# Four first blocks over four pairs of loads, and an order planned with each pool tile's turn

## The chip, the cores and the metric

The kernel runs on one core of a Trainium2 chip. Its time is the device time of one execution, in microseconds (us). Five engines run their own instruction queues side by side: TensorE (PE, matrix products), VectorE (DVE) and ScalarE (ACT, both elementwise), GpSimd (POOL, almost unused here) and SyncE (SP), which here issues nearly all DMAs. A matmul reads two operands from the on-chip memory and accumulates into a bank of PSUM, 128 partitions of 512 floats.

## The reference

Two branches share their input and are mixed by a gate:

```python
    x = A_q
    g = _sigmoid((x * gate_w).sum(-1, keepdims=True))
    a = _A_ref(x, A_k, A_v, A_shift_k, A_ssm_k, A_ssm_D)
    b = _B_ref(x, B_w1, B_w2)
    return g * a + (1 - g) * b
```

Branch b is the dense one, relu(x w1) w2 for 2048 rows of 512 values, with an inner width of 1792. Branch a shifts k with four taps, multiplies it by v, convolves each channel over the whole sequence with `ssm_k` (by an FFT of twice the length), adds kv times `ssm_D` and multiplies by q. All is in 32-bit floats.

## The kernel before, in words

**Dense branch.** The rows are worked on in 4 chunks of 512, and the inner width in 14 blocks of 128. For chunk c and block f the first product ("m_c_f", 12 matmuls of 128x512, L353 to L355) goes to one of four shared PSUM banks, tag "cv". ACT takes the relu to a rounded high part hh (L365), DVE the rest hl (L368), which gives the bank free. The second product (12 matmuls, L380 to L382) adds to four banks of its own, m_c_0 to m_c_3, that are kept over the 14 blocks. For precision every operand is split: a copy to a rounded format is the high part (names with h, cast on ACT, L268), and what is left is the low part (names with l, DVE, L271); three matmuls (high by high, high by low, low by high) make one product. x, w1 and w2 are split on the chip, once for the weights.

**Head.** The blocks below G of chunk 0 are treated apart, since nothing is on the chip yet: their w1 columns come in an own array `wf` (`load_first`, L303, with casts gh at L316 and low parts gl at L319), and `mlp1_first` (L337) goes over the four pieces k of the 512 input values in the outer loop, so that it can start with the first piece of x and of weights. Thirteen matmuls on zeros (L737) run ahead of it. G is 2 before the change.

**Convolution.** It is a factored Fourier transform by small ("tiled") matmuls of 32 or 64 partitions. DVE forms the shifted k times v in tiles acc and tmp (conv_x); stage 1 (s1x of acc, s1h of the filter, L416, eight chunks each) fills all four "cv" banks in one run; ACT copies them to ev tiles (L426), which are stored and read back in another layout (r). In 8 rounds, the forward transforms f_h and f_x (L519) follow, then products on DVE in tiles z, u and xs (L533, copies L543), then the inverse iv (L613), again to four banks, copied by ACT to bv (L623), stored, read back, transformed once more (y, L714) and gated. These runs stand between dense matmuls.

**The order.** The program lists all operations with their engine, estimated duration, dependencies, rank, and what they take and give of each pool; `Plan.order` simulates the engines and always issues the ready operation of least rank. The kernel is emitted in that order, and each engine runs its own part of it strictly in that order. Room is a count by tag: an operation may be placed when enough tiles of its tag are free. The pool itself hands out the tiles of one tag in turn: the next tile is the one that has been given back longest ago in program order, and who takes it waits for that one's last user. Most work tiles (x, in, acc, tmp, ev, r, z, u, xs, bv, and so on) are one common tag, "a", 14 tiles of 128x1024 floats; the counts for ev, z and the others are caps on their share of it. A table of numbers sets the ranks, the pool sizes and caps, and margins (SAFE) that the planner adds to a time.

Of the kernel before, what the change touches and what calls it, by code (L numbers as in the profile page):

```python
# [8 lines left out]
F32 = mybir.dt.float32  # L9
F32R = mybir.dt.float32r  # L10
# [4 lines left out]
P = 128  # L15
# [64 lines left out]
class Plan:  # L80
# [3 lines left out]
    def __init__(self, room):  # L84
        self.room, self.ops, self.turn = dict(room), [], {}

# [13 lines left out]
    def order(self):  # L100
# [4 lines left out]
        out, soon, mode = [], [], False  # L105
# [9 lines left out]
        while True:  # L115
            for eng, ops in ready.items():
# [4 lines left out]
                if eng == "PE" and any(o["rank"][0] == 1 and not o["take"] for o in ops):  # L121
                    held = {"cv" for o in ops + (soon if SOON else []) if o["tiles"] and len(o["take"]) >= HOLD and all(self.turn[q][0] == o["n"] for q in o["fifo"])
                            and all(t == "cv" or self.room[t] >= o["take"].count(t) for t in o["take"])}
                for op in ops:
                    if best is not None and op["rank"] >= best["rank"]:
                        continue
                    if any(self.room[t] <= op["take"].count(t) - 1 for t in op["take"]):
                        continue
                    if any(self.turn[q][0] != op["n"] for q in op["fifo"]):
                        continue  # L130
                    if op["rank"][0] and any(t in held for t in op["take"]):
                        continue
                    if op["dma"] and pipe > now + DMA_AHEAD:
                        continue
                    best = op
# [4 lines left out]
                for t in op["take"]:  # L140
                    self.room[t] -= 1
                for q in op["fifo"]:
                    self.turn[q].pop(0)
# [20 lines left out]
            while events and events[0][0] <= now + 1e-9:  # L164
# [6 lines left out]
                if what == "done":  # L171
                    for t in op["give"]:
                        if isinstance(t, list):

                            t[0] -= 1
                            for name in () if t[0] else t[1:]:
                                self.room[name] += 1
                        else:
                            self.room[t] += 1
# [19 lines left out]
def act_time(n, psum=False):  # L199
    return n * 0.000833 + (0.17 if psum else 0.195)  # L200


def dve_time(n):
    return n * 0.001042 + 0.15
# [8 lines left out]
def build(tc, wf, xp, qn, kn, vn, hn, dn, sh, gw, w1, w2, cs1, ccc, cib, out):  # L213
# [20 lines left out]
    plan = Plan(room)  # L234
# [9 lines left out]
    def double(key, kind):  # L244
        T[key] = cpool[0].tile([P, 2 * D], F32, tag="a", bufs=AB, name=kind + "_" + "_".join(map(str, key)))
        return T[key]
# [56 lines left out]
    def load_first(ks, rank):  # L303
        n = G * P

        def load():
            w = double(("wf", ks[0]), "wf")
            nc.sync.dma_start(w[:, :len(ks) * n], wf[:, ks[0] * n:(ks[-1] + 1) * n])
            for i, k in enumerate(ks):
                T["g", k] = w[:, i * n:(i + 1) * n]  # L310

        ld = add("SP", ISSUE["SP"], rank, load, (), ["a", "ev"], dma=ROW * G // 4 * len(ks))
        free = [len(ks), "a", "ev"]
        for k in ks:
            def h(k=k):
                (nc.vector.tensor_copy if k == 0 else nc.scalar.copy)(tile_of(("g", "h", k), f"gh{k}", w=G * P, dt=F32R, p=wp), T["g", k])  # L316

            def l(k=k):
                nc.vector.tensor_tensor(tile_of(("g", "l", k), f"gl{k}", w=G * P, dt=F32R, p=wp), T["g", k], T["g", "h", k].bitcast(F32), op=OP.subtract)  # L319

            a = add("DVE", dve_time(G * P), -2000, h, [ld]) if k == 0 else add("ACT", act_time(G * P), -2000 + k, h, [ld])
            wdone["g", k] = add("DVE", dve_time(G * P), -2000 + k, l, [a], (), [free])
            wdone["gh", k] = a
# [6 lines left out]
    def mlp1_first():  # L330
        prev = [None] * G
        for k in range(4):
            for n, (a, b) in enumerate((("h", "h"), ("h", "l"), ("l", "h"))):
                for f in range(G):
                    def go(k=k, f=f, n=n, a=a, b=b):
                        ps = bank(("m1", 0, f)) if k == n == 0 else T["m1", 0, f]
                        mm(ps, part(a, f, k), T["x", b, 0, k], start=k == n == 0, stop=k == 3 and n == 2)  # L337

                    prev[f] = add("PE", MM, (1, -9, k, n), go, [(wdone["gh", k], xhigh[0, k]), (xdone[0, k],), (wdone["g", k],)][n] + (prev[f],),
                                  ["cv"] if k == n == 0 else ())  # L340
        for f in range(G):
            mlp1_out(0, f, prev[f])
# [400 lines left out]
    load_first((0,), -1002.5)  # L743
    load_first((1, 2, 3), -1001.5)
# [43 lines left out]
G = 2  # L788
# [7 lines left out]
SAFE = dict(PE0=0.3, PE1=0.175, ACT=0, DVE=0.4)  # L796
# [6 lines left out]
IN = 5  # L803
EV = 4
ACC = 2
TMP = 3
# [4 lines left out]
UB = 2  # L811
XSB = 1
CIB = 1
BVB = 3
EVI = [0, 0, 0, 0]
RK = {'H': -6, 'X': 4.5, 'Y': 0, 'I': 6}
HOLD = 4
SOON = 1
BRB = 6
QB = 2  # L820
# [3 lines left out]
EVR = 0  # L824
CWG = 8
# [3 lines left out]
BB = 3  # L829
X0 = -25.0  # L830
XP = 17.0
H0 = -20.0
# [43 lines left out]
```

## Time and profile before

Three runs took 405.32, 405.39 and 407.22 us, median 405.39. The profiled execution took 404.28 us by its own time; its span from first to last instruction is 402.1 us.

| what | value |
|---|---|
| span of the profiled execution | 402.1 us |
| its own time | 404.28 us |
| PE busy | 392.0 us (97%) |
| DVE busy | 287.7 us (72%) |
| ACT busy | 139.1 us (35%) |
| granted TensorE clock, mean | 0.999 |
| bytes moved by DMA | 93.52 MB, mean 233 GB/s |
| last dense product of the head (L337) ends, L353 starts | 12.43 us |
| last matmul starts | 398.03 us |

The names are the program's tiles, without buffer numbers. Busy times of PE overlap, since matmuls are pipelined: the distance between two starts is what one costs. "idle before <-" names what released an engine after it stood still.

### The profile page before, as it was taken

How to read it: one execution, taken by the hardware profiler on the slowest of the kernel's cores; microseconds unless marked ns; L12 is line 12 of the kernel's file. 1: busy time of each engine (PE TensorE's matmuls, PEld its weight loads, DVE VectorE, ACT ScalarE, POOL GpSimd, SP SyncE). 2: the span in 40 equal slices, each digit the busy share in tenths (PEclk: the TensorE clock that was granted, in tenths of full speed). 3: DMA queues.
4: the chain of work that ended last, by engine and by line, in shares of the span. 5: the costliest groups of instructions: out<-in, count | busy, mean ns of one | idle time of the engine just before them, and what ended most of it. 6: DMA issues, size and time to landing. Idle time of an engine off the chain costs nothing.

```text
span 402.1 us, 6451 instructions
## 1 busy us (share of the span) xinstructions
PE 392.0 (97%) x2509; PEld 268.3 (67%) x2509; DVE 287.7 (72%) x446; ACT 139.1 (35%) x263; POOL 1.4 (0%) x6
## 2 busy tenths in 40 slices
PE   7999999899999999999999999999998999999996
PEld 5878777578667666658556456474665786777774
DVE  4699999782897762279889797897989523664753
ACT  4553443344443343234343333323434520101110
POOL 0000000000000000000000000000000000000000
PEclk9999999999999999999999999999999999999999
DMA  7989668776677966674664829456393658987702
GB/s 253 373 311 332 224 213 297 266 256 253 210 261 260 343 253 221 225 291 128 223 174 166 269 89 300 121 217 182 148 251 149 210 164 316 387 319 282 261 0 104
DMA packets 39231, 93.52 MB, mean 233 GB/s; under 512 B 3841, under 2 KB 6289, under 8 KB 39202
## 3 DMA queue, kind: packets, MB, share of 16 engines
q1 hardware_dynamic: 39138, 93.08, 67.3%
q8 instruction: 19, 0.31, 0.3%
q0 software_dynamic: 64, 0.05, 0.1%
q14 instruction: 10, 0.08, 0.0%
HBM read 60.61 MB, written 32.51 MB: 232 GB/s over the span
## 4 chain that ended last, share of the span: by engine, by line
PE 90%; DMA 4%; DVE 2%; ACT 1%; SPq 1%; issue 1%; DVEq 0%; ACTq 0%
PE m L380 13%; PE m L353 13%; PE m L381 12%; PE m L382 12%; PE m L354 12%; PE m L355 12%; PE iv L613 3%; PE f_h L519 3%; PE f_x L519 3%; PE s1h L416 2%; PE y L714 2%; PE s1x L416 2%; DMA q_qs<-qn 2%; DMA wf_wf<-wf 1%; PE m L337 1%; DMA sa<-ev_evsh 1%
## 5 line engine op out<-in xcount | busy, mean ns | idle before, releaser
L380 PE MATMUL m<-w1h_h,hh 128*128 128x512 f32 x224 | 91.1, 407 | 0.0
L381 PE MATMUL m<-w1l_l,hh 128*128 128x512 f32 x224 | 87.5, 391 | 0.0
L382 PE MATMUL m<-w1h_h,hl 128*128 128x512 f32 x224 | 87.3, 390 | 0.0
L368 DVE SCALAR_TENSOR_TENSOR hl<-m,hh 128x512 fp32r<-128x512 f32 x56 | 38.6, 690 | 63.8 <-ACT hh L365 63.4
L365 ACT ACTIVATE hh<-m 128x512 fp32r<-128x512 f32 x56 | 33.4, 598 | 134.1 <-PE m L355 131.6
L353 PE MATMUL m<-xh_h,w0h_h 128*128 128x512 f32 x192 | 77.1, 402 | 2.0 <-ACT ev_evsx L426 1.6
L354 PE MATMUL m<-xl_l,w0h_h 128*128 128x512 f32 x192 | 75.0, 390 | 0.0
L355 PE MATMUL m<-xh_h,w0l_l 128*128 128x512 f32 x192 | 74.9, 390 | 0.0
L380 PEld LDWEIGHTS m<-w1h_h,hh 128*128 128x128 f32 x224 | 42.0, 188 | 34.7 <-issue 27.0
L353 PEld LDWEIGHTS m<-xh_h,w0h_h 128*128 128x128 f32 x192 | 36.0, 188 | 23.4 <-issue 6.7
L382 PEld LDWEIGHTS m<-w1h_h,hl 128*128 128x128 f32 x224 | 42.1, 188 | 9.0
L381 PEld LDWEIGHTS m<-w1l_l,hh 128*128 128x128 f32 x224 | 42.1, 188 | 7.5
L355 PEld LDWEIGHTS m<-xh_h,w0l_l 128*128 128x128 f32 x192 | 36.1, 188 | 7.7
L354 PEld LDWEIGHTS m<-xl_l,w0h_h 128*128 128x128 f32 x192 | 36.1, 188 | 6.8
L481 DVE TENSOR_TENSOR acc_acc<-acc_acc,tmp_tmp 128x1024 f32<-128x1024 f32 x24 | 29.4, 1224 | 0.7
L623 ACT COPY bv_bvs<-iv 128x512 f32<-128x512 f32 x30 | 15.7, 602 | 28.2 <-PE iv L613 16.1
L478 DVE TENSOR_TENSOR tmp_tmp<-in_k,sht_sht 128x512 f32<-128x512 f32 x32 | 21.3, 687 | 1.7 <-DMA in_k<-kn 1.6
L426 ACT COPY ev_evsx<-s1x 128x512 f32<-128x512 f32 x30 | 15.7, 599 | 18.9 <-PE s1x L416 16.1
L426 ACT COPY ev_evsh<-s1h 128x512 f32<-128x512 f32 x32 | 16.5, 601 | 13.3 <-PE s1h L416 10.6
L543 ACT COPY xs_xs<-f_x 128x512 f32<-128x512 f32 x24 | 13.5, 590 | 19.2 <-PE f_x L519 19.2
L533 DVE TENSOR_TENSOR z_pz<-f_x,z_hz 128x512 f32<-128x512 f32 x16 | 10.3, 687 | 11.8 <-PE f_x L519 11.8
L519 PE MATMUL f_x<-r_r_x,cw 64*32 64x512 f32 x256 | 16.7, 599 | 0.0
(70 smaller groups left out, 391.7 us busy)
## 6 DMA issues: line engine op xcount, KB each, us to landing
sa<-ev_evsh SPq DMA_DIRECT2D x16, 512.0 KB, 4.9
sa<-ev_evsx SPq DMA_DIRECT2D x16, 512.0 KB, 3.4
r_r_h<-sa SPq DMA_DIRECT2D x16, 512.0 KB, 5.7
r_r_x<-sa SPq DMA_DIRECT2D x16, 512.0 KB, 6.8
sb<-bv_bvs SPq DMA_DIRECT2D x32, 256.0 KB, 3.7
br_br<-sb SPq DMA_DIRECT2D x16, 512.0 KB, 6.7
raw<-w SPq DMA_DIRECT2D x26, 256.0 KB, 4.4
in_k<-kn SPq DMA_DIRECT2D x10, 512.0 KB, 6.4
```

The costliest lines, as they stand in the source:

```text
L353: mm(ps, part("h", f, k), T["x", "h", c, k], start=k == 0, stop=False)
L354: mm(ps, part("h", f, k), T["x", "l", c, k], start=False, stop=False)
L355: mm(ps, part("l", f, k), T["x", "h", c, k], start=False, stop=k == 3)
L365: nc.scalar.activation(tile_of(("hh", c, f), "hh", dt=F32R, p=mp, bufs=HHB), T["m1", c, f], AF.Relu)
L368: nc.vector.scalar_tensor_tensor(tile_of(("hl", c, f), "hl", dt=F32R, p=mp, bufs=HHB), T["m1", c, f], 0.0, T["hh", c, f].bitcast(F32), op0 ...
L380: mm(ps, T["hh", c, f][:, z], T["w", "h", 1, f], start=f == 0, stop=False)
L381: mm(ps, T["hh", c, f][:, z], T["w", "l", 1, f], start=False, stop=False)
L382: mm(ps, T["hl", c, f][:, z], T["w", "h", 1, f], start=False, stop=f == NF - 1)
L426: (nc.vector.tensor_copy if dve else nc.scalar.copy)(T["ev" + t, c, i], T["s1" + t, c, i])
L478: nc.vector.tensor_tensor(o[:, z], T["k", c + (j == 0) + part][:, u], T["sht", j // 2][:, j % 2 * D:(j % 2 + 1) * D], op=OP.mult)
L481: nc.vector.tensor_tensor(T["acc", c], T["acc", c], T[dst], op=OP.add)
L519: mm(ps[b][32 * j:32 * j + 32, :], T[k("cw")][at, 64 * j + 32 * o:64 * j + 32 * o + 32], T[k("r", t, j // 2)][at, (j % 2) * D:(j % 2 + 1) ...
```

## The change

Three things are changed.

1. `Plan` is given the list of tags that are only caps. For every other tag (the common pool "a", raw, x, hh, the PSUM banks and some more) it now keeps the tiles in the order in which the program gives them back. An operation is placed only when the tiles whose turn it is are free in the simulation (`fits`); before, any free tiles were enough.
2. The head takes four blocks (G = 4) in place of two. The weights come in four loads of 128x512 (256 KB), each following the load of the x piece that goes with it; before there were one of 128 KB and one of 384 KB. The first piece is cast on DVE in two halves. `mlp1_first` has 48 matmuls in place of 24, and in its last piece k = 3 it finishes block after block.
3. The table of numbers is another, and the order is planned anew with it. The numbers of dense and of small matmuls are the same as before (24 dense ones only move from `mlp1` to `mlp1_first`), and lines below `Plan` have moved: in the changed kernel the head's matmuls are L365, the first product L381 to L383, the second L408 to L410, s1x L444, f L547, iv L641, casts L291 and L294, gh L340, ev copies L454, bv copies L651.

```diff
+    def __init__(self, room, caps):
         self.room, self.ops, self.turn = dict(room), [], {}
+        self.tiles = {t: [[0]] * n for t, n in room.items() if t not in caps}
+
+    def fits(self, op, but=()):
+        for t in set(op["take"]) - set(but):
+            n = op["take"].count(t)
+            if self.room[t] < n or t in self.tiles and any(x[0] for x in self.tiles[t][:n]):
+                return False
+        return True
...
-                    if any(self.room[t] <= op["take"].count(t) - 1 for t in op["take"]):
+                    if not self.fits(op):
                         continue
...
                 for t in op["take"]:
                     self.room[t] -= 1
+                    if t in self.tiles:
+                        self.tiles[t].pop(0)
+                op["frees"] = []
+                for g in op["give"]:
+                    if isinstance(g, list):
+
+                        g[0] -= 1
+                        op["frees"].append(pending.setdefault(id(g), [0]))
+                        op["frees"][-1][0] += 1
+                        names = () if g[0] else g[1:]
+                    else:
+                        op["frees"].append([1])
+                        names = (g,)
+                    for t in names:
+                        self.room[t] += t in self.tiles
+                        op["frees"][-1].append(t)
+                        if t in self.tiles:
+                            self.tiles[t].append(op["frees"][-1])
...
-    plan = Plan(room)
+    plan = Plan(room, ("in", "acc", "tmp", "ev", "r", "z", "u", "xs", "bv", "br", "t", "b", "q"))
...
-    def load_first(ks, rank):
+    def load_first(k, rank):
         n = G * P
 
         def load():
...
+            T["g", k] = double(("wf", k), "wf")[:, :n]
+            nc.sync.dma_start(T["g", k], wf[k])
+
+        ld = add("SP", ISSUE["SP"], rank, load, (), ["a", "ev"], dma=ROW * G // 4)
+        parts = 2 if k == 0 else 1
...
-            for n, (a, b) in enumerate((("h", "h"), ("h", "l"), ("l", "h"))):
-                for f in range(G):
+            for n, f in [(n, f) for n in range(3) for f in range(G)] if k < 3 else [(n, f) for f in range(G) for n in range(3)]:
...
     for k in range(4):
         load_x(0, k, -1000 + k)
-    load_first((0,), -1002.5)
-    load_first((1, 2, 3), -1001.5)
+        load_first(k, -1002.5 + k)
...
-G = 2
+G = 4
...
-EVI = [0, 0, 0, 0]
+EVI = [0, 0, 0, 1]
...
-        "wf": w1[:, :, :G].transpose(1, 0, 2, 3).reshape(P, 4 * G * P),
+        "wf": w1[:, :, :G].reshape(4, P, G * P),
```

With EVI, one of the four bv copies of each of the first seven iv runs goes to DVE.

The order on SP at the start of the program, before (x_x is a piece of x, wf_wf of the first weights, raw a block of w1 or w2):

```order
L290 DMA x_x_0_76<-xp 128x512
L308 DMA wf_wf_78<-wf 128x256
L290 DMA x_x_1_94<-xp 128x512
L308 DMA wf_wf_96<-wf 128x768
L290 DMA x_x_2_98<-xp 128x512
L290 DMA x_x_3_102<-xp 128x512
L264 DMA raw_0_106<-w 128x512
```

and in the changed kernel:

```order
L313 DMA x_x_0_76<-xp 128x512
L331 DMA wf_wf_78<-wf 128x512
L313 DMA x_x_1_94<-xp 128x512
L331 DMA wf_wf_96<-wf 128x512
L313 DMA x_x_2_98<-xp 128x512
L331 DMA wf_wf_102<-wf 128x512
L313 DMA x_x_3_104<-xp 128x512
L287 DMA raw_0_110<-w 128x512
L287 DMA raw_1_116<-w 128x512
L287 DMA raw_2_123<-w 128x512
L331 DMA wf_wf_133<-wf 128x512
```

The first weights have grown from two loads to four, and the fourth stands behind three raw blocks.

The order on PE at the first s1x run of the program, before (the numbers in m_0_2 and m_0_3 with w1 are the second product's banks; m_0_9 with xh is the first product of block 9):

```order
L381 MATMUL m_0_3_231<-w1l_l_7_444,hh_7_573 128x512
L382 MATMUL m_0_3_231<-w1h_h_7_424,hl_7_585 128x512
L416 MATMUL s1x_0_620<-acc_acc_305,s1c_s1t 64x512
L416 MATMUL s1x_1_621<-acc_acc_305,s1c_s1t 64x512
L416 MATMUL s1x_2_622<-acc_acc_305,s1c_s1t 64x512
L416 MATMUL s1x_3_623<-acc_acc_305,s1c_s1t 64x512
...
L380 MATMUL m_0_0_213<-w1h_h_8_442,hh_8_597 128x512
L381 MATMUL m_0_0_213<-w1l_l_8_466,hh_8_597 128x512
```

and in the changed kernel:

```order
L409 MATMUL m_0_3_258<-w1l_l_5_298,hh_5_425 128x512
L410 MATMUL m_0_3_258<-w1h_h_5_284,hl_5_439 128x512
L444 MATMUL s1x_0_498<-acc_acc_305,s1c_s1t 64x512
L444 MATMUL s1x_1_499<-acc_acc_305,s1c_s1t 64x512
L444 MATMUL s1x_2_500<-acc_acc_305,s1c_s1t 64x512
L444 MATMUL s1x_3_501<-acc_acc_305,s1c_s1t 64x512
...
L381 MATMUL m_0_6_523<-xh_h_0_100,w0h_h_6_317 128x512
L382 MATMUL m_0_6_523<-xl_l_0_106,w0h_h_6_317 128x512
```

The run stands after 157 dense matmuls in place of 217, and a first product follows it where a second product did. The second s1x run stands after 253 in place of 274, with the first product m_0_10 right behind it; the third after 298 in place of 382, with three matmuls of a second product behind it.

The order on ACT around the last iv copies of chunk 2, before (xs_xs is a copy of f_x, o keeps a finished bank of the second product):

```order
L268 CAST xh_h_3_2953<-raw_3_1782 128x512
L543 COPY xs_xs_7_2927<-f_x_1_7_2873 128x512
L623 COPY bv_bvs_6_2998<-iv_6_2968 128x512
L623 COPY bv_bvs_6_3004<-iv_6_2970 128x512
L388 COPY o_3011<-m_2_0_1872 128x512
L388 COPY o_3014<-m_2_1_1880 128x512
L623 COPY bv_bvs_6_2998<-iv_6_2969 128x512
```

and in the changed kernel:

```order
L291 CAST xh_h_3_2998<-raw_3_1910 128x512
L717 ACT_TABLE_LOAD
L717 ACTIVATE gwt_gwt<-gwt_gwt 128x1 x2
L651 COPY bv_bvs_7_3041<-iv_7_3010 128x512
L651 COPY bv_bvs_7_3041<-iv_7_3011 128x512
L416 COPY o_3057<-m_2_0_1987 128x512
L416 COPY o_3062<-m_2_1_1996 128x512
```

The inverse at this place is the last one (round 7) in place of round 6, and the last xs copies stand well ahead of it.

More of the change, by code (lines that the diff above doesn't have):

```diff
@@ L80 @@
 class Plan:
-    def __init__(self, room):
+    def __init__(self, room, caps):
         self.room, self.ops, self.turn = dict(room), [], {}
+        self.tiles = {t: [[0]] * n for t, n in room.items() if t not in caps}
[5 more added lines that the diff above has]
+        return True
     def add(self, eng, dur, rank, fn, deps=(), take=(), give=(), dma=0, fifo=(), tiles=False, store=False):
@@ L104, in order @@
         pipe = 0.0
-        out, soon, mode = [], [], False
+        out, soon, mode, pending = [], [], False, {}
         for op in self.ops:
@@ L122, in order @@
                     held = {"cv" for o in ops + (soon if SOON else []) if o["tiles"] and len(o["take"]) >= HOLD and all(self.turn[q][0] == o["n"] for q in o["fifo"])
-                            and all(t == "cv" or self.room[t] >= o["take"].count(t) for t in o["take"])}
+                            and self.fits(o, ("cv",))}
                 for op in ops:
@@ L171, in order @@
                 if what == "done":
[L172 to L179, printed above, removed]
+                    for x in op["frees"]:
+                        x[0] -= 1
+                        for t in () if x[0] else x[1:]:
+                            self.room[t] += t not in self.tiles
                 for o in op["next"]:
@@ L301, in load_w, with h, l @@
                              lambda: tile_of(("w", "l", i, f), f"w{i}l{f}", dt=F32R, bufs=1, p=wp), (), ["raw"])
-    def load_first(ks, rank):
+    def load_first(k, rank):
         n = G * P
         def load():
[L307 to L323, printed above, removed]
+            T["g", k] = double(("wf", k), "wf")[:, :n]
+            nc.sync.dma_start(T["g", k], wf[k])
+        ld = add("SP", ISSUE["SP"], rank, load, (), ["a", "ev"], dma=ROW * G // 4)
+        parts = 2 if k == 0 else 1
+        for i in range(parts):
+            def h(i=i):
+                if i == 0:
+                    tile_of(("g", "h", k), f"gh{k}", w=n, dt=F32R, p=wp)
+                z = slice(i * n // parts, (i + 1) * n // parts)
+                (nc.vector.tensor_copy if k == 0 else nc.scalar.copy)(T["g", "h", k][:, z], T["g", k][:, z])
+            a = add("DVE", dve_time(n // parts), (-2000, k), h, [ld]) if k == 0 else add("ACT", act_time(n), (0, -999.5 + k), h, [ld])
+            for f in range(i * G // parts, (i + 1) * G // parts):
+                wdone["gh", k, f] = a
+        def l():
+            nc.vector.tensor_tensor(tile_of(("g", "l", k), f"gl{k}", w=n, dt=F32R, p=wp), T["g", k], T["g", "h", k].bitcast(F32), op=OP.subtract)
+        wdone["g", k] = add("DVE", dve_time(n), (0, -999.5 + k), l, [a], (), ["a", "ev"])
     def part(h, f, k):
@@ L331, in mlp1_first, with go @@
         prev = [None] * G
+        prod = (("h", "h"), ("h", "l"), ("l", "h"))
         for k in range(4):
-            for n, (a, b) in enumerate((("h", "h"), ("h", "l"), ("l", "h"))):
-                for f in range(G):
[L335 to L340, printed above, removed]
+            for n, f in [(n, f) for n in range(3) for f in range(G)] if k < 3 else [(n, f) for f in range(G) for n in range(3)]:
+                def go(k=k, f=f, n=n):
+                    ps = bank(("m1", 0, f)) if k == n == 0 else T["m1", 0, f]
+                    a, b = prod[n]
+                    mm(ps, part(a, f, k), T["x", b, 0, k], start=k == n == 0, stop=k == 3 and n == 2)
+                prev[f] = add("PE", MM, (1, -9, k, *((f, n) if k == 3 else (n, f))), go,
+                              [(wdone["gh", k, f], xhigh[0, k]), (xdone[0, k],), (wdone["g", k],)][n] + (prev[f],), ["cv"] if k == n == 0 else ())
         for f in range(G):
@@ L795 @@
 LAG = dict(PE=0.2, ACT=0.05, DVE=0.06, POOL=0.15)
-SAFE = dict(PE0=0.3, PE1=0.175, ACT=0, DVE=0.4)
+SAFE = dict(PE0=0.6, PE1=0.175, ACT=0, DVE=0.4)
 QUEUE = dict(s1="SP", iv="SP", b="SP")
@@ L802 @@
 OB = 2
-IN = 5
-EV = 4
+IN = 6
+EV = 3
 ACC = 2
-TMP = 3
+TMP = 2
 RB = 4
@@ L810 @@
 ZB = 7
-UB = 2
-XSB = 1
+UB = 1
+XSB = 2
 CIB = 1
-BVB = 3
-EVI = [0, 0, 0, 0]
-RK = {'H': -6, 'X': 4.5, 'Y': 0, 'I': 6}
-HOLD = 4
+BVB = 2
+EVI = [0, 0, 0, 1]
+RK = {'H': 0, 'X': 4.5, 'Y': 0, 'I': 4.5}
+HOLD = 2
 SOON = 1
-BRB = 6
-QB = 2
+BRB = 4
+QB = 4
 AB = 14
@@ L823 @@
 EVL = [0, 0, 1, 1]
-EVR = 0
-CWG = 8
+EVR = 1
+CWG = 15
 LASTF = 2
@@ L828 @@
 YG = 0
[L829 to L832, printed above, removed]
+BB = 2
+X0 = -32.0
+XP = 24.0
+H0 = -30.0
 W0 = -100
```

## The prediction

> **What bounds the kernel now.** I read the page's busy table first, then its chain of waits, then the list of what TensorE (PE) waited for, and then the timeline of each place named there.
>
> ```profile
> span 402.1 us, 6451 instructions
> PE 392.0 (97%) x2509; PEld 268.3 (67%) x2509; DVE 287.7 (72%) x446; ACT 139.1 (35%) x263; POOL 1.4 (0%) x6
> PE 90%; DMA 4%; DVE 2%; ACT 1%; SPq 1%; issue 1%; DVEq 0%; ACTq 0%
> PE m L353 <- ACT bv_bvs L623: 1.7, 1, 1.7
> PE m L353 <- ACT ev_evsx L426: 1.6, 1, 1.6
> PE m L337 <- ACT gh_h L316: 1.6, 1, 1.6
> PE warm L737 <- DVE zero_zero L732: 1.2, 1, 1.2
> PE m L353 <- DVE hl L368: 0.4, 1, 0.4
> ```
>
> PE is the bound: it holds 90% of the chain. Its waits are five single events, not a rhythm. The amount of matmul work is not changed, so all that can be won is in these five, and all that can be lost is in new ones of the same kind. Durations below are from this one execution, which took 404.28 us; the median of the runs shown is 405.39 us, 1.1 us more. I work out a difference and apply it to both.
>
> **The steady price of a matmul** comes from this stretch of PE's timeline:
>
> ```profile
> 12.43 0.39 PE L353 MATMUL m<-xh_h,w0h_h 128*128 128x512 f32 x1
> 13.11 0.39 PE L353 MATMUL m<-xh_h,w0h_h 128*128 128x512 f32 x1
> 13.79 0.39 PE L353 MATMUL m<-xh_h,w0h_h 128*128 128x512 f32 x1
> ```
>
> Three matmuls lie between neighbouring rows, so six take 1.36 us: 0.227 us each.
>
> **The head, before.** PE's timeline, then ACT's, DVE's and SP's:
>
> ```profile
> 4.27 1.19 PE L337 MATMUL m<-xh_h,gh_h 128*128 128x512 f32 x2
> 5.26 0.87 PE L337 MATMUL m<-xl_l,gh_h 128*128 128x512 f32 x2
> 5.96 0.62 PE L337 MATMUL m<-xh_h,gl_l 128*128 128x512 f32 x2
> 8.16 0.50 PE L337 MATMUL m<-xh_h,gh_h 128*128 128x512 f32 x1 [1.58 <-ACT gh_h L316]
> ...
> 3.83 0.29 DVE L316 CAST gh_h<-wf_wf 128x256 fp32r<-128x256 f32 x1 [2.69 <-DMA wf_wf<-wf]
> 5.84 0.62 ACT L268 CAST xh_h<-x_x 128x512 fp32r<-128x512 f32 x1 [1.70 <-DMA x_x<-xp]
> 7.71 1.02 ACT L316 CAST gh_h<-wf_wf 128x256 fp32r<-128x256 f32 x3 [1.24 <-DMA wf_wf<-wf]
> ...
> 10.00:12.00 2.00, 2.00 (x11) 1.63 (x10) 2.00 (x4) 1.83 (x4) 0.00 (x0) 1.00 1.05 423
> ```
>
> The 24 matmuls from 4.27 to 12.43 took 8.16 us where 24 x 0.227 = 5.44 would do: 2.7 us lost, 1.75 of it before 8.16 (the two from 5.96 could have been followed at 6.41), where the 384 KB piece of weights was awaited. The next 24 follow without a gap, so the 48th ends near 12.43 + 5.44 = 17.87.
>
> The landings give what the loads allow: 393 KB (x and 128 KB of weights, in thousands of bytes) were there at 3.83, 655 at 5.84, 1049 at 7.71. In the new order x and wf of 262 KB each alternate, so k = 0 needs 524 KB: by interpolation 3.83 + 2.01 x 131/262 = 4.8 us. Two half casts of 0.29 and a short hand-over put the first matmul at about 5.3, one us later than now. From there 12 matmuls at a time take 2.72 us: k = 0 to 8.0. The second weights are the 1049th KB, 7.7, and their cast on ACT of 512 columns takes 0.62 (the row at 5.84): k = 1 from about 8.45 (0.45 us lost), k = 2 from 11.2, k = 3 from 13.9. The fourth weights are the 11th load, behind three raw tiles, the 2621st KB; from some 1573 KB at 9.1 us at the 423 GB/s of the last row (windows: the last number) that is 11.6, and up to 12.3 with the slower rates around. Cast by 12.9 and its low half on DVE by 13.7, so k = 3 is not held up. The 48th ends at 13.9 + 2.72 = 16.6: 1.25 us earlier than 17.87. The bounds: the fourth weights 1.2 us later would eat all of it; k = 0 on time would give 1.6. I take 1.05, because of the slow first matmuls below.
>
> **The slow first matmuls.** This is the list of PE's L737 and L337 by line, minimum, median, maximum in ns:
>
> ```profile
> L737 PE MATMUL warm<-zero_zero x13: 415/415/580, 1.2 to 3.9; 128*128 128x256 f32 x13
> L337 PE MATMUL m<-xh_h,gh_h x8: 390/396/766, 4.3 to 11.3; 128*128 128x512 f32 x8
> L337 PE MATMUL m<-xl_l,gh_h x8: 389/397/629, 5.3 to 11.8; 128*128 128x512 f32 x8
> ```
>
> The warm-up starts 13 matmuls of 256 columns within 2.7 us, 0.22 each, as long as 512 columns take later. So PE runs at half its rate there, though the granted clock shows 1.00. The first two L337 starts are 0.5 us apart, and from 5.96 on they are 0.23. In the new order PE idles from the warm-up's end (4.27) to 5.3. If this restarts its slow time, up to 12 matmuls of k = 0 cost 0.45 rather than 0.227, 2.7 us more, less the 0.45 already lost there. [...]
>
> **The three later waits.** PE, then ACT, at the three places:
>
> ```profile
> 72.93 0.39 PE L382 MATMUL m<-w1h_h,hl 128*128 128x512 f32 x1
> 74.94 0.50 PE L353 MATMUL m<-xh_h,w0h_h 128*128 128x512 f32 x1 [1.63 <-ACT ev_evsx L426]
> ...
> 229.51 0.50 PE L353 MATMUL m<-xh_h,w0h_h 128*128 128x512 f32 x1 [0.39 <-DVE hl L368]
> ...
> 307.98 0.40 PE L382 MATMUL m<-w1h_h,hl 128*128 128x512 f32 x1
> 310.03 0.50 PE L353 MATMUL m<-xh_h,gh_h 128*128 128x512 f32 x1 [1.65 <-ACT bv_bvs L623]
> ...
> 74.31 1.07 ACT L426 COPY ev_evsx<-s1x 128x512 f32<-128x512 f32 x2 [2.68 <-DMA sa<-ev_evsh]
> 309.39 1.15 ACT L623 COPY bv_bvs<-iv 128x512 f32<-128x512 f32 x2 [5.26 <-DVE z_hz L533]
> ```
>
> At 74.94 a first product needs a bank that holds an s1x result. Its ACT copy stood 2.68 us for a tile in pool "a" whose last user, the store of ev_evsh, had not ended. At 310.03 the same holds for a bank of iv: ACT stood 5.26 us for a tile of "a" that the products with z_hz still read. In both another tile was free by count, but the pool hands them out in turn. The losses against a steady 0.227: 2.01 - 0.23 = 1.78, and 2.05 - 0.23 = 1.82. The planner counts by turn after the change, so such a copy is set where its tile is free by its own costs. I take both off whole (bounds: 0 to 3.6 for the pair), since in the new order the first bank wait after the last iv of chunk 2 has its copies ahead of the o copies, and DVE has ended z products some 3.8 us earlier by my count. The 0.43 at 229.51 (a hidden part late by a queue position) goes too; it was one coincidence, and hl stands elsewhere now.
>
> **What is added.** One tiled run more (51 stretches of small matmuls where there were 50). Its price and that of a new wait come from an s1x run of before, PE and ACT:
>
> ```profile
> 153.94 0.39 PE L382 MATMUL m<-w1h_h,hl 128*128 128x512 f32 x1
> 154.26 1.11 PE L416 MATMUL s1x<-acc_acc,s1c_s1t 32*64 32x512 f32 x16
> 155.30 0.50 PE L380 MATMUL m<-w1h_h,hh 128*128 128x512 f32 x1
> 155.64 0.40 PE L381 MATMUL m<-w1l_l,hh 128*128 128x512 f32 x1
> ...
> 155.43 2.06 ACT L426 COPY ev_evsx<-s1x 128x512 f32<-128x512 f32 x4 [2.50 <-PE s1x L416]
> ```
>
> Going in costs 0.32 - 0.23 = 0.09, coming out 0.34 - 0.23 = 0.11, and splitting a run adds the like at its seam: 0.4 us as an upper value.
>
> The new wait: s1x takes all four shared banks. In the row above second products follow, which need none of them. In the new order the first two s1x runs are followed at once by a first product (m_0_6, and the same at m_0_10). It can start only when the first copy has ended: 155.43 + 2.06/4 = 155.95, plus a hand-over, 156.05, against 155.30. That is 0.75 us, twice: 1.5. Three second products between, as at all such places before, hide 0.68 of it, and the third new place has those. At m_0_6 the copy also stands on ACT behind the casts of w0_9, w1_9 and w0_10, whose loads may land late: 0 to 1.3 more, I take 0.3. Below nothing isn't possible: the bank cannot be free before its copy.
>
> Next is DVE, whose share in the first chunk is near full:
>
> ```profile
> 22.00:32.00 10.00, 10.00 (x46) 8.28 (x45) 9.38 (x13) 5.14 (x10) 0.00 (x0) 1.00 0.99 360
> 52.00:62.00 10.00, 10.00 (x56) 7.39 (x55) 9.76 (x12) 4.31 (x8) 0.00 (x0) 1.00 0.63 223
> ```
>
> DVE (third number) works 9.4 to 9.8 us of 10, and DMA is 99% busy around 27 us. The k-v products must now be ready earlier: s1x comes after 157 and 253 dense matmuls, where it came after 217 and 274, so up to 60 x 0.227 = 13.6 us earlier. By the price of DVE's rows in its new order the first has some 6 us of slack, the second 2.5, and hl_6 none to speak of: 0.2.
>
> The extra half cast (one more DVE instruction, 0.29) lies inside the wait for x; the bv copy on DVE per iv (0.69, eight times) lies in the idle us that DVE has in each 17.5 us round of the forward part, with about 0.7 us to spare before the bank is wanted: nothing, or 8 x 0.2 if that cover is gone.
>
> **Sum:** -1.05 - 1.78 - 1.82 - 0.43 + 0.4 + 1.5 + 0.3 + 0.2 = -2.7 us: 401.6 for an execution like the profiled one, 402.7 against the median.
>
> **Rivals.**
> - The gain is eaten in the first chunk. The two bank waits at 2 us each rather than 0.75, and hl_6 and hl_7 late by 0.5: +2.7 - 0.5 over the sum, so about 404.9. For it: DVE and DMA near full there; against: ACT is 43% busy there.
> - The turns are followed, but by costs that are not the chip's, so the waits at 72 and 308 come back elsewhere: +3.6 to the sum, 406.3, still within half a per cent or just past it. For it: the planner knew the stores' times before as well. Against: the two waits named a tile whose turn it was, which it did not model.
> - PE's slow start again: +2.2, less what I took (0.2): 404.7. For it, the rows above; against, 3 us of warm-up lie right ahead.
> - Slower. DVE and DMA cannot feed the convolution so early. The k and v loads (512 KB each) queue behind weights while DMA is 99% busy; from 2.5 us late on at the second s1x, each us is a us of PE. Three runs there, 6 us late at the second and third, would cost 2 x 3.5 = 7: 409. For it the 9.76 of 10; against the slack of 6 at the first.
>
> **Chances.** Forecast 0.57 (its own range 400.8 to 404.2), eaten 0.15, turns 0.08, slow start 0.07, slower 0.09; 0.04 is left for better than the sum (both bank waits covered: 401.0). What a measurement here can tell is 0.5%, 2.0 us: faster means under 403.4. Of the forecast's 0.57 about 0.5 lies there, with the 0.04: 0.54, and 0.02 of the eaten: 0.56. Slower means over 407.4: the 0.09 and a fifth of the turns: 0.11. The rest, 0.33, is no change. The range reaches from the better case to just over the turns: 400.2 to 406.2.
>
> **What would show it.** First L365 near 5.3 us, the first L381 near 16.6; no PE wait on bv_bvs, and none over 1 us on ev_evsx late in chunk 0; two of about 0.75 on ev_evsx at the matmuls of m_0_6 and m_0_10. Starts 0.45 apart after 5.3 would show the slow PE; a PE wait on acc or DVE L396 of over 2 us would make the forecast wrong.

## The result, and the profile after

The changed kernel takes 401.56 us (median of 6 runs, 399.37 to 403.04) against 406.02 us for the kernel before (6 runs beside it, 403.98 to 407.22). The ratio is 0.9886, 95% interval 0.9842 to 0.9931: 1.1% faster, 4.5 us. The profiled executions differ by as much: 404.28 and 399.70 us, spans 402.1 and 397.8.

The page of the changed kernel, its span, busy times and chain, and then what PE waited for:

```profile
span 397.8 us, 6443 instructions
PE 390.7 (98%) x2509; PEld 268.1 (67%) x2509; DVE 292.0 (73%) x452; ACT 136.8 (34%) x254; POOL 1.4 (0%) x6
PE 97%; DMA 1%; ACT 0%; DVE 0%; DVEq 0%; issue 0%
...
PE m L381 <- ACT ev_evsx L454: 1.4, 2, 0.7
PE warm L765 <- DVE zero_zero L760: 1.2, 1, 1.2
PE m L365 <- DVE gh_h L340: 0.8, 1, 0.8
```

PE's share of the chain goes from 90% to 97%. The waits for bv_bvs (1.7), for hl (0.4) and for the head's weights on ACT (1.6) are gone, and of ev_evsx two short ones are left. PE's timeline at the head and at the two new places:

```profile
1.19 3.06 PE L765 MATMUL warm<-zero_zero 128*128 128x256 f32 x13 [1.19 <-DVE zero_zero L760]
5.07 1.16 PE L365 MATMUL m<-xh_h,gh_h 128*128 128x512 f32 x4 [0.82 <-DVE gh_h L340]
6.08 1.08 PE L365 MATMUL m<-xl_l,gh_h 128*128 128x512 f32 x4
...
7.90 1.07 PE L365 MATMUL m<-xh_h,gh_h 128*128 128x512 f32 x4
...
15.83 0.39 PE L365 MATMUL m<-xh_h,gl_l 128*128 128x512 f32 x1
16.06 0.39 PE L408 MATMUL m<-w1h_h,hh 128*128 128x512 f32 x1
...
40.45 1.11 PE L444 MATMUL s1x<-acc_acc,s1c_s1t 32*64 32x512 f32 x16
42.26 0.50 PE L381 MATMUL m<-xh_h,w0h_h 128*128 128x512 f32 x1 [0.70 <-ACT ev_evsx L454]
...
65.50 1.11 PE L444 MATMUL s1x<-acc_acc,s1c_s1t 32*64 32x512 f32 x16
67.31 0.50 PE L381 MATMUL m<-xh_h,w0h_h 128*128 128x512 f32 x1 [0.70 <-ACT ev_evsx L454]
```

From 5.07 on nothing stops the head, and the 49th dense matmul starts at 16.06 in place of 17.87. Behind both s1x runs 1.81 us pass where 1.04 would do.

The account by PE's starts, in us. A loss is what a step took beyond the steady 0.227; for a run of small matmuls the steps into it and out of it are counted together (the median of such runs). In brackets stands the start of the last matmul or run ahead of the wait:

| place | before | after | difference |
|---|---|---|---|
| start of the 49th dense matmul | 17.87 | 16.06 | -1.81 |
| wait for an ev tile (72.93) | 1.78 | none | -1.78 |
| wait for hl (228.03) | 0.43 | none | -0.43 |
| wait for a bv tile (307.98) | 1.82 | none | -1.82 |
| first product right behind s1x, twice | none | 0.77 each | +1.54 |
| one 32-matmul run cut into two of 16 | 2.10 | 2 x 1.24 | +0.38 |
| start of the last matmul | 398.03 | 393.70 | -4.33 |

The rows above the last add up to -3.92; the other 0.41 is spread over many steps, none of which I took apart. Behind the last matmul both need 4.1 us to the end of the span.

### The profile page after: what moved, and what is told of

It reads as the page before. It is cut to its first block, busy times and chain, and to the rows that moved or that the text cites. A ratio compares the mean times of both kernels' runs of the same rounds, so it can differ in the third digit from the quotient of the medians.

```text
span 397.8 us, 6443 instructions
## 1 busy us (share of the span) xinstructions
PE 390.7 (98%) x2509; PEld 268.1 (67%) x2509; DVE 292.0 (73%) x452; ACT 136.8 (34%) x254; POOL 1.4 (0%) x6
## 4 chain that ended last, share of the span: by engine, by line
PE 97%; DMA 1%; ACT 0%; DVE 0%; DVEq 0%; issue 0%
PE m L408 14%; PE m L381 13%; PE m L409 13%; PE m L410 13%; PE m L383 12%; PE m L382 12%; PE f_x L547 4%; PE iv L641 4%; PE f_h L547 4%; PE m L365 3%; PE s1x L444 2%; PE s1h L444 2%; PE y L742 2%; DMA x_x<-xp 1%; ACT ev_evsx L454 0%; DVE xl_l L294 0%
## 5 line engine op out<-in xcount | busy, mean ns | idle before, releaser
L408 PE MATMUL m<-w1h_h,hh 128*128 128x512 f32 x224 | 90.8, 405 | 0.0
L410 PE MATMUL m<-w1h_h,hl 128*128 128x512 f32 x224 | 87.2, 389 | 0.0
L381 PE MATMUL m<-xh_h,w0h_h 128*128 128x512 f32 x160 | 64.4, 403 | 1.4 <-ACT ev_evsx L454 1.4
L408 PEld LDWEIGHTS m<-w1h_h,hh 128*128 128x128 f32 x224 | 42.0, 187 | 33.1 <-issue 25.4
L382 PE MATMUL m<-xl_l,w0h_h 128*128 128x512 f32 x160 | 62.4, 390 | 0.0
L383 PE MATMUL m<-xh_h,w0l_l 128*128 128x512 f32 x160 | 62.4, 390 | 0.0
L410 PEld LDWEIGHTS m<-w1h_h,hl 128*128 128x128 f32 x224 | 42.1, 188 | 9.1
L381 PEld LDWEIGHTS m<-xh_h,w0h_h 128*128 128x128 f32 x160 | 30.0, 187 | 21.4 <-issue 4.2
L383 PEld LDWEIGHTS m<-xh_h,w0l_l 128*128 128x128 f32 x160 | 30.0, 188 | 6.5
L382 PEld LDWEIGHTS m<-xl_l,w0h_h 128*128 128x128 f32 x160 | 30.1, 188 | 5.6
L454 ACT COPY ev_evsh<-s1h 128x512 f32<-128x512 f32 x32 | 16.6, 601 | 18.3 <-PE s1h L444 18.3
L651 ACT COPY bv_bvs<-iv 128x512 f32<-128x512 f32 x23 | 12.0, 595 | 27.9 <-PE iv L641 21.4
L454 ACT COPY ev_evsx<-s1x 128x512 f32<-128x512 f32 x30 | 15.8, 598 | 16.0 <-PE s1x L444 16.0
L381 PE MATMUL m<-xh_h,gh_h 128*128 128x512 f32 x48 | 19.2, 400 | 0.0
L382 PE MATMUL m<-xl_l,gh_h 128*128 128x512 f32 x48 | 18.7, 390 | 0.0
```

What stands on the lines that cost most here:

```text
L381: mm(ps, part("h", f, k), T["x", "h", c, k], start=k == 0, stop=False)
L382: mm(ps, part("h", f, k), T["x", "l", c, k], start=False, stop=False)
L383: mm(ps, part("l", f, k), T["x", "h", c, k], start=False, stop=k == 3)
L408: mm(ps, T["hh", c, f][:, z], T["w", "h", 1, f], start=f == 0, stop=False)
L410: mm(ps, T["hl", c, f][:, z], T["w", "h", 1, f], start=False, stop=f == NF - 1)
L454: (nc.vector.tensor_copy if dve else nc.scalar.copy)(T["ev" + t, c, i], T["s1" + t, c, i])
```

## The experiments

**Both kernels again.** The executions of one kernel differ by more than a timing error: the spans of twelve executions of the changed kernel lie at 397.6 to 398.4 (5) and 399.5 to 400.4 (7). The changed kernel again:

> The changed kernel once more, beside the three below: a span of 397.8 and the same waits (0.8 head, twice 0.7 behind ev copies), to see how far one execution differs from another.

It took 401.36 us, and its ratio to the kernel before was 0.9885 (0.9852 to 0.9918). The profiled execution was of the longer group, span 400.3, with the same three waits. Its head is not the same:

```profile
5.10 2.05 PE L365 MATMUL m<-xh_h,gh_h 128*128 128x512 f32 x4 [0.78 <-DVE gh_h L340]
6.95 1.91 PE L365 MATMUL m<-xl_l,gh_h 128*128 128x512 f32 x4
8.66 1.91 PE L365 MATMUL m<-xh_h,gl_l 128*128 128x512 f32 x4
10.36 1.16 PE L365 MATMUL m<-xh_h,gh_h 128*128 128x512 f32 x4
11.36 1.08 PE L365 MATMUL m<-xl_l,gh_h 128*128 128x512 f32 x4
```

The first product starts at the same time, but the first twelve come 0.44 us apart, until 10.36; then the pace is that of the first execution. The 49th dense matmul starts at 18.64, 2.58 us later than in the first execution, so here the head is 0.77 us behind the 17.87 of the kernel before. The granted clock does not show it: its mean over the span is 0.999, and in the run with 6 matmuls on zeros below, which has the same first twelve, it is 1.00 in every window from 2 to 14 us. The span is 2.5 us longer too, so the two groups are taken for executions with and without this head; only one of each was traced. This is the slow start that the prediction had as a rival.

The kernel before, again:

> The kernel before, once more. Its runs lie in two groups, spans of about 402 with a mean clock of 0.999 and of about 404.3 with 0.994 or 0.995. Theory A (a wait of TensorE of 1.6 to 2 us, in the executions in which it falls right, lets the rate drop to half, and the next 3 to 5 us cost 2): if this execution is of the second group, the granted clock is under 0.9 in one or two windows right behind one of the waits at 8.2, 74.9 or 310 us, and 1.00 elsewhere. Rival B: the clock is a little lower all along.

It took 408.89 us; span 405.9, mean clock 0.992: of the second group. PE's timeline at the head and in the middle, and the windows around the wait there (the granted clock is the third number from the end):

```profile
7.92 1.06 PE L337 MATMUL m<-xh_h,gh_h 128*128 128x512 f32 x2 [1.40 <-ACT gh_h L316]
8.78 1.06 PE L337 MATMUL m<-xl_l,gh_h 128*128 128x512 f32 x2
...
74.21 0.39 PE L382 MATMUL m<-w1h_h,hl 128*128 128x512 f32 x1
76.91 0.80 PE L353 MATMUL m<-xh_h,w0h_h 128*128 128x512 f32 x1 [2.31 <-ACT ev_evsx L426]
77.50 0.63 PE L354 MATMUL m<-xl_l,w0h_h 128*128 128x512 f32 x1
79.20 0.63 PE L355 MATMUL m<-xh_h,w0l_l 128*128 128x512 f32 x1
79.95 0.39 PE L354 MATMUL m<-xl_l,w0h_h 128*128 128x512 f32 x1
...
76.00:77.00 1.00, 0.10 (x1) 0.10 (x1) 0.96 (x2) 0.73 (x2) 0.00 (x0) 0.70 0.98 334
77.00:78.00 1.00, 1.00 (x3) 0.81 (x4) 0.64 (x1) 0.82 (x2) 0.00 (x0) 0.50 0.13 49
79.00:80.00 1.00, 1.00 (x4) 0.77 (x4) 0.00 (x0) 0.00 (x0) 0.00 (x0) 0.59 1.03 293
80.00:82.00 2.00, 2.00 (x11) 1.65 (x10) 0.09 (x1) 0.72 (x2) 0.00 (x0) 1.00 0.28 106
```

Theory A holds. The wait itself is 2.3 us here, and behind it the clock is at half for some 3.3 us, with matmuls 0.43 apart: the seven steps from 76.91 to 79.95 take 3.04 where 7 x 0.227 = 1.59 would do, 1.45 us more. The head's wait, 1.40 us, does the same to the matmuls from 7.92 on in this execution (granted clock 0.53 from 8 to 10 us): the 18 matmuls that are left of the head take 5.80 where 4.08 would do, and the 49th starts at 19.16 instead of 17.87. The wait for bv, 1.6 us, does not: the clock is 1.00 behind it. So a wait that the change removes was worth its length, and in part of the executions half as much again or more. Of the 43 executions of the kernel before that ran beside the experiments, 24 have mean clocks of 0.987 to 0.996 and spans of 403.3 to 407.3, and 19 have 0.998 or more and 401.1 to 403.3.

**The gap ahead of the first product closed.** Sixteen matmuls on zeros are issued, and the order stays as it was:

```diff
     def warm():
-        for _ in range(WARM):
+        for _ in range(16):
```

> The changed kernel in its own order, with 16 matmuls on zeros in place of 13, so that they end at about 5.05 us, where the first product starts. Seen so far: in the profiled execution of the changed kernel the 48 matmuls of the head followed each other at 0.23 from 5.07 on (span 397.8), in another execution of the same kernel the first 12 were 0.45 apart until 10.4 (span 400.3); the six runs beside each lie in two groups, 397.6 to 398.4 and 399.5 to 400.4. [...]

```profile
1.19 3.74 PE L765 MATMUL warm<-zero_zero 128*128 128x256 f32 x16 [1.19 <-DVE zero_zero L760]
5.17 1.17 PE L365 MATMUL m<-xh_h,gh_h 128*128 128x512 f32 x4 [0.25 <-DVE gh_h L340]
```

All six spans lie at 397.9 to 398.6, where the shorter group of the changed kernel has 397.6 to 398.4; the second group is gone. The median is 400.35, the ratio 0.9874 (0.9845 to 0.9903). A gain in the median is not shown: the medians differ by 1.0 to 1.2, but on different chips, and the ratios to the kernel before (0.9874, and 0.9885 for the changed kernel) by 0.4 us, with intervals that overlap. What the run shows is that six of six executions are of the shorter group, where five of twelve were. That three matmuls more, and not the closed gap, did this is ruled out further down, where the gap is closed without them. What sets the slow executions of one kernel apart, no trace here shows.

**Fewer matmuls on zeros.** WARM = 6 in the table:

> The changed kernel with 6 in place of 13 matmuls on zeros ahead of the head, so that they end at about 2.6 us and TensorE idles 2.4 us before its first product at 5.07. [...]

```profile
1.19 1.65 PE L765 MATMUL warm<-zero_zero 128*128 128x256 f32 x6 [1.19 <-DVE zero_zero L760]
5.10 2.05 PE L365 MATMUL m<-xh_h,gh_h 128*128 128x512 f32 x4 [2.26 <-DVE gh_h L340]
...
10.35 1.52 PE L365 MATMUL m<-xh_h,gh_h 128*128 128x512 f32 x4
```

The first twelve took 5.25 us where the first execution of the changed kernel took 2.83, and the 49th started at 18.99 where it started at 16.06. But this is one execution, and its first twelve are those of the changed kernel's longer group (5.10 to 10.36) to a hundredth: it does not tell a cause in the shorter warm-up from the slow start that 13 matmuls leave as well. And it took 423.91 us: the planner reads WARM as well, and it made another order, in which PE waits for ev_evsx 2.8, 2.5 and 1.7 us and the clock falls to 0.70 behind the first of these. I had not foreseen that. Only the head of this run is read.

**The head alone.** The new head with G = 4, but the other numbers of before and planning by counts:

```diff
-    plan = Plan(room, ("in", "acc", "tmp", "ev", "r", "z", "u", "xs", "bv", "br", "t", "b", "q"))
+    plan = Plan(room, tuple(room))
...
+G = 4
...
+EV = 4
+EVI = [0, 0, 0, 0]
```

> The head of four blocks over four pairs of loads with the numbers of before (but G = 4) and the order planned by counts. Theory A (the head's gain is its own, 2.04 us at the 48th matmul): the 49th matmul starts at 15.8 instead of 17.9 as in the changed kernel, and the rest of the program keeps waits like those of before, so the span is about 400. Rival B (the head is faster, but the order behind it is not tuned to it and gives it back: DVE was over 93% busy from 22 to 72 us and cannot follow two us earlier): 49th matmul at 15.8 all the same, but new waits of TensorE in the first 100 us, span 401.5 or more.

It took 410.17 us (407.06 to 411.89), ratio 1.0105 (1.0059 to 1.0150): slower than before. PE's waits:

```profile
PE m L381 <- ACT ev_evsx L454: 6.2, 5, 2.6
PE m L381 <- ACT bv_bvs L651: 1.8, 1, 1.8
```

In its profiled execution the 49th dense matmul started at 16.16, 1.7 us earlier than before, and the rest gave it back: five waits of 6.2 us in all for ev_evsx, and the wait for bv at 313 as before. Rival B is right in kind; it had put the new waits into the first 100 us, and the two longest (1.5 and 2.6) end at 101 and 118.

**Two blocks over four pairs.** The kernel before, with its first weights in four loads of 128 KB:

```diff
-    load_first((0,), -1002.5)
-    load_first((1, 2, 3), -1001.5)
+    for k in range(4):
+        load_first((k,), -1002.5 + k)
```

> The kernel before with two blocks in the head, its weights in four contiguous loads of 128 KB, each behind its piece of x, in place of one of 128 and one of 384 KB. Theory A (half of the head's loss was that the second to fourth pieces came as one load, which is there only as a whole): the second piece can be multiplied when some 786 KB are there, 6.5 us instead of 8.16; the 25th matmul starts at 10.7 to 11.2 instead of 12.43, and the first waits after it are under 0.5 us. Rival B (six matmuls for each 393 KB loaded, 1.36 us of work for 1 us of load, leave no room, and the bytes of the rows of 1 KB land slower): 25th matmul at 12 or later. The two waits at 72.9 and 308 us stay in both, span 400.5 (A) or 402 (B).

```profile
9.94 0.61 PE L337 MATMUL m<-xh_h,gl_l 128*128 128x512 f32 x2
11.07 0.50 PE L353 MATMUL m<-xh_h,w0h_h 128*128 128x512 f32 x1 [0.52 <-ACT w0h_h L268]
```

The 25th matmul starts at 11.07 in place of 12.43, as in theory A, though it waits 0.52 for the next weights. Of the 1.36 us, 0.62 are left at the 49th (17.25), and nothing at the end (last matmul at 397.95; 405.72 us, ratio 1.0000, 0.9975 to 1.0026), since its wait for ev_evsx is 2.1 in place of 1.6. The span, 402.2, is the one that rival B had. So half of the head's loss of 2.7 us came with the single load of 384 KB; its size and its layout in memory changed together here, and the run does not part them; that rows of 1 KB land slower, which rival B put in, was not shown. With four blocks each pair brings PE 2.72 us of work, and in the changed kernel no later piece was waited for.

**The new numbers, planned by counts.** Only the one line with `tuple(room)` of the head's experiment, on the changed kernel:

> The changed kernel (head of four blocks, new numbers), but the order is planned by counts again: any free tile of a pool counts, its turn is not asked for. Theory A (planning by turns removed the two waits at 72.9 and 308 us, 1.78 + 1.82): with the count only, at least one wait of TensorE of 1 us or more behind a copy that waits for its tile of the common pool comes back, and the span is 399.5 to 403 instead of 397.8. Rival B (the new numbers place the work so that the turns do not matter): the same waits as in the changed kernel (0.8 at the head, 0.7 twice behind ev copies) and no other, span within 0.6 of 397.8.

405.41 us, ratio 0.9976 (0.9941 to 1.0010). Of its ten executions the profiled one took 2202.86 us, and its trace tells nothing of the order; the spans of the others are 401.0 to 403.7. The same kernel was profiled once more:

> New numbers with the order planned by counts, once more: its profiled execution was a disturbed one, its nine others had spans of 401.0 to 403.7 against 397.6 to 400.4 of the changed kernel. Theory A (a tile whose turn has not come holds a copy, and TensorE waits behind it): one or more waits of TensorE behind ACT copies, 1.5 to 3.5 us in all, beyond the two of 0.7 at m_0_6 and m_0_10. Rival B (TensorE's waits are those of the changed kernel, and what is longer lies behind the last matmul): last matmul at 393.5 to 396 and 3 us or more between there and the end beyond the 4.3 of the changed kernel.

```profile
PE m L381 <- ACT ev_evsx L454: 1.4, 2, 0.7
PE m L365 <- DVE gh_h L340: 0.9, 1, 0.9
...
396.87 0.39 PE L410 MATMUL m<-w1h_h,hl 128*128 128x512 f32 x1
...
398.05 0.75 DVE L677 SCALAR_TENSOR_TENSOR t_ts<-m,gwt_gwt,t_ts 128x512 f32<-128x512 f32 x1
399.62 0.88 DVE L677 SCALAR_TENSOR_TENSOR t_ts<-m,gwt_gwt,t_ts 128x256 f32<-128x256 f32 x2
```

PE's waits are those of the changed kernel, and no tile wait has come back: theory A failed in both texts, though five of the nine spans lie where its first text had put them. Rival B has the waits right; its first text was wrong on the span (within 0.6 of 397.8), and the second put the loss in the right place but at 3 us or more, where 2.4 were found. The last matmul starts 0.6 us later than in the changed kernel's execution with the same slow head (396.87 against 396.26), and 2.4 us come behind it: DVE still has gate products to do and ends at 400.5, 6.4 us from the last matmul to the end instead of 4.1. The forward transforms stand later in this order (first f_h at 167.9 instead of 157.3 in the execution with the same head), and with them the last y run, at 393.05 instead of 380.9. Why planning by counts puts them later was not followed up. By the ratios to the kernel before (0.9976 and 0.9885) the turns are worth some 3 to 4 us with the new numbers, and these lie at the end of the program, not in the waits that I had given them.

**The turns alone.** The planner by turns with the numbers and the head of before:

> The kernel before with its own numbers and its own head of two blocks, planned by turns. Theory A (turns alone remove the two waits): 402.1 - 1.78 - 1.82 = 398.5 us span, no TensorE wait over 1 us but the head's. Rival B (an operation that is refused because its tile's turn has not come is placed later, and with these numbers that costs more than the waits did, in the stretch up to 150 us or at the end): no wait for a tile, but other waits of TensorE (for hl, for banks after s1x) or a later end after the last matmul; span 403 to 410.

427.96 us, ratio 1.0542 (1.0495 to 1.0588). PE's waits, the windows around the longest, and what SP and DVE did there:

```profile
PE m L376 <- ACT ev_evsx L449: 14.0, 5, 5.0
...
136.00:141.00 5.00, 0.05 (x1) 0.05 (x1) 1.96 (x2) 0.69 (x2) 0.00 (x0) 0.72 0.30 109
141.00:146.00 5.00, 5.00 (x14) 3.94 (x15) 2.94 (x3) 1.41 (x4) 0.00 (x0) 0.60 0.73 247
...
133.69 0.89 SPq L453 DMA_DIRECT2D sa<-ev_evsh  x2
139.01 1.23 DVE L498 TENSOR_TENSOR acc_acc<-in_k,sht_sht 128x1024 f32<-128x1024 f32 x1 [6.42 <-issue]
140.31 2.05 ACT L449 COPY ev_evsx<-s1x 128x512 f32<-128x512 f32 x4 [6.16 <-issue]
```

DVE stood 6.4 us and ACT 6.2, and DVE went on about when the stores issued at 133.69 would be done by their median of 4.4 us in this run. In this place the profile names no releaser; two other waits of DVE for an acc tile in this run, 6.6 us in all, it puts down to the store of ev_evsh. Then PE ran at 0.60 for 5 us. Rival B was right in sign and short in size (403 to 410 expected). A likely reason lies in the planner's costs, though I did not test it: with no other transfer ahead it gives a store of 512 KB 0.47 + 0.6 + 524288/390000 + 0.3 = 2.7 us, and the pages of the profile show medians of 4.4 and 3.3 for the two kinds in this run, 4.7 and 3.8 in the changed kernel. An order that asks for a tile just when its store ends by these costs would ask too early.

**s1x three matmuls earlier.** Each of the two waits had been put down to the time of the first copy, so three matmuls of a second product were put between:

```diff
     issued = plan.order()
+    pe = [o for o in issued if o["eng"] == "PE"]
+    for i in range(1, len(pe) - 1):
+        m2, s1, m1 = pe[i - 1:i + 2]
+        if s1["take"] == ("cv",) * 4 and s1["rank"][0] == 0 and m1["take"] == ("cv",) and not m2["tiles"] and len(m2["rank"]) == 3 and not m2["take"]:
+            issued.remove(m2)
+            issued.insert(issued.index(s1) + 1, m2)
```

> The changed kernel, with the last three matmuls of a second product moved from just ahead of the first two s1x runs to just behind them, so that a first product no longer follows s1x at once. Theory A (the two waits of 0.77 us are the copy's time, 0.75, and three matmuls of 0.227 cover 0.68 of it): the wait at m_0_10 goes to under 0.1; that at m_0_6 goes to about 0.35, since ACT has casts until 41.2 there; span 397.8 - 1.1 = 396.7. Rival B (what is late is something behind, DVE's hl or the filled banks, so the wait only moves): the span stays within 0.4 of 397.8.

```profile
42.31 1.11 PE L444 MATMUL s1x<-acc_acc,s1c_s1t 32*64 32x512 f32 x16
43.36 0.50 PE L408 MATMUL m<-w1h_h,hh 128*128 128x512 f32 x1
43.93 0.39 PE L410 MATMUL m<-w1h_h,hl 128*128 128x512 f32 x1
44.33 0.50 PE L381 MATMUL m<-xh_h,w0h_h 128*128 128x512 f32 x1
```

The wait is gone at the first place but for 0.17 (0.40 from 43.93 to 44.33), and wholly at the second. The profile was of the slow head; its span of 399.2 is 1.1 us under the 400.3 of the changed kernel with that head. The six spans are 396.7 to 399.2, and the median is 400.25 (ratio 0.9858, 0.9823 to 0.9893), 1.1 us under the changed kernel's 401.36 on the same chip. The intervals of the two ratios overlap, but waits, traces and medians agree: theory A.

**And the first weights first.** The same, and on DVE the cast halves of the first weights ahead of the first low part of x:

```diff
+    dve = [o for o in issued if o["eng"] == "DVE"]
+    i = next(i for i, o in enumerate(dve) if o["rank"] == (-2000, 0))
+    issued.remove(dve[i - 1])
+    issued.insert(issued.index(dve[i + 1]) + 1, dve[i - 1])
```

> As the one before, and the first weights' cast halves on DVE stand ahead of the first low part of x. In the changed kernel the cast starts at 4.64, just when DVE is done with xl, so the trace does not show when the weights landed. Theory A (they landed earlier, about 4.2, and DVE's order holds the first matmul): first matmul at 4.7 to 4.8 instead of 5.07, and the end as much earlier, 396.4. Rival B (they landed at 4.6): first matmul at 5.0 to 5.1, or xl now comes later and holds the fifth matmul: no gain, up to 0.3 lost.

```profile
4.11 0.49 DVE L340 CAST gh_h<-wf_wf 128x256 fp32r<-128x256 f32 x2 [2.98 <-DMA wf_wf<-wf]
...
4.55 1.66 PE L365 MATMUL m<-xh_h,gh_h 128*128 128x512 f32 x4 [0.22 <-DVE gh_h L340]
6.05 1.09 PE L365 MATMUL m<-xl_l,gh_h 128*128 128x512 f32 x4
```

The first weights were there by 4.11, and DVE's order had held the first matmul by half a us: theory A's start. Its end is not shown. The first four matmuls take 1.50 us where they took 1.01, and the 49th starts at 16.07, a hundredth later than in the first execution of the changed kernel, so the half us is not gained here. What is gained is the longer group: the gap is 0.22, the slow start is over with the first four, and all six spans lie at 396.5 to 397.9; 399.39 us, ratio 0.9832 (0.9800 to 0.9863). This closes the gap with the same 13 matmuls on zeros, so in these runs the second group hangs on the gap (0.82 and 0.78 us in the changed kernel, 0.25 and 0.22 us in the two versions up to here that do not have the group) and not on the amount of warm-up.

**All three.** With 14 matmuls on zeros:

> The changed kernel with three edits: s1x ahead of the last three matmuls of a second product at its first two places, the first weights' casts ahead of the low part of x, and 14 matmuls on zeros, which end where the first product starts (4.55 us). Theory A (each edit keeps what it showed alone): spans 396.0 to 397.0 without a second group, 0.3 to 0.5 us under the version with 13. Rival B (14 delay the first product when they run slow): 397 or more.

398.92 us (398.65 to 399.24), ratio 0.9839 (0.9809 to 0.9869), spans 396.7 to 397.3. There is no second group, as theory A had it, but no gain over the version with 13 that the intervals could show. In the profiled execution the first product started at 4.91, and rival B's delay is not the reason: the 14th matmul ended at 4.54, and PE waited another 0.37 for the cast, which DVE began at 4.47, when the weights had landed. The 49th started at 16.09. By their ratios both versions lie some 2 us under the changed kernel, at 0.9885; the intervals overlap a little, and on the chip that it shared with the version of 13 the medians are 401.36 and 399.39.

## Why the prediction was right or wrong

The time was inside the range and its sign was right; the forecast was a gain of 2.7 us, and 4.5 were measured, 4.3 between the two traces. Of the 1.6 us between forecast and traces the head made 0.76, the two additions that did not come 0.5, and the rest is the 0.41 that no row names. Step by step:

- **PE is the bound, and only its few single waits count.** Right. The account of the starts closes to 0.41 us with them, the head and one run more.
- **The head, -1.05.** Mis-sized: -1.81 in the profiled execution. The landings were taken from before by their bytes; the second weights, put at 7.7, were cast from 6.87 on, and the second piece had no stall in place of 0.45. The first matmul was put at 5.3 and started at 5.07; the weights, put at 4.8, were there by 4.11 in the run that cast them first, and here DVE took them up at 4.64, behind the low part of x. The 0.2 that I took off for the slow start was wrong in both kinds of execution (0.1 in one, some 2.6 in the other).
- **The slow start, chance 0.07, up to +2.2.** Undervalued most of all. It came in 7 of 12 executions by their spans, and cost 2.58 us at the 49th matmul in the one that was traced, more than the 2.2 of the rival. Against it I had put the warm-up that lies right ahead. The runs show that a gap of 0.8 us behind the warm-up leaves the slow start in part of the executions, and that by their spans none of the 18 executions of the three versions with gaps of 0.22 to 0.37 us has it; what decides within one kernel no trace shows. In the median the error hides, by luck: the kernel before loses in a like way behind its longer waits, by the clocks in 24 of 43 executions (in the traced one the granted clock was 0.50 from 77 to 79 us), which I did not see in its one profile, where the clock was 1.00 behind each of them.
- **The two tile waits, -3.6, whole.** Their size was right, and they are gone. The reason as put ("the planner counts by turn after the change, so such a copy is set where its tile is free") failed: with the new numbers planned by counts they are gone too, and with the old numbers planned by turns ev_evsx waits 14.0 us. With the new head and the old numbers by counts the wait for bv stays and ev_evsx waits 6.2 us, so what removed the two waits is the new numbers, and that my -3.6 came out is luck. What the turns gave, beside the new numbers planned by counts, is the 3 to 4 us at the end of the program, for which the prediction had no term. The new numbers with the old head were not run. The rival "the turns are followed, but by costs that are not the chip's" would fit what the old numbers do, though that was not tested; in the changed kernel it did not strike.
- **hl, -0.43.** Right.
- **One more tiled run, +0.4 as an upper value.** Right: 0.38.
- **The two new bank waits, +1.5.** Right to 0.04: 0.77 each, at m_0_6 and m_0_10, and the order alone and one copy's row had told them. The +0.3 for the casts ahead of the copy at m_0_6 was nothing: the casts ended in time, and the copies began at 41.62, when PE had filled the banks.
- **DVE, +0.2 for hl_6, and the slower rival.** Nothing: no wait on DVE is in the list but the head's. The products for s1x were ready where it stood.

## What to carry to other kernels

Where one engine is the bound, count its single waits, look in the order for the same pattern at new places, and price each by one row: this closed the account to 0.41 of 4.33 us here. An order, the costs it was planned with and the numbers tuned on it are one thing: each half alone was slower than the start, or no faster. A forecast term can come out for another reason than the one given, and only a run with one part of the change shows it. Read more than one execution before a row is taken as the rule: a gap of 0.8 us ahead of the first product cost 2.6 us more in one execution than in another, and waits of 1.4 and 2.3 us, once they had halved the clock, cost 1.5 to 1.7 more. Filling the gap with matmuls on zeros delayed nothing in the traced execution: they ended 0.25 us ahead of the first product.

## What the runs showed of the hardware

In these runs PE's rate did not stay fixed once it was up, and the length of a wait alone did not decide. In one execution of the kernel before, waits of 1.40 and 2.31 us took the granted clock to 0.53 and 0.50 for some 3.3 us each, and one of 1.65 us at 313 us left it at 1.00. In another execution a wait of 1.63 us, at the place of the 2.31, left it at 1.00, and so did one of 2.6 us in the kernel with the new head alone. At the start of the program the first matmuls of 512 columns came 0.50 and then 0.35 us apart until 5.96 in the first execution of the kernel before, and 0.43 to 0.46 us apart until 10.36 in the second execution of the changed kernel, against 0.23 later. The view of the granted clock shows 1.00 from 0 to 14 us in that execution of the kernel before, and from 2 to 14 us in the run with 6 matmuls on zeros, which was slow until 10.35, so the slow stretch at the start had to be read from the starts.
